# Attention and two expert layers on one core: joined float32 groups, another opening order, and weight forms held behind a unit's evictions

## The chip, the cores and the metric

The program runs on one NeuronCore of one Trainium2 chip. The metric is the device time of one execution in microseconds (us). TensorE (PE; its weight loads are PEld), VectorE (DVE), ScalarE (ACT), GpSimd (POOL) and SyncE (SP, which issues nearly all DMAs) each take their instructions in order from a queue of their own.

## The reference, cut to what matters

```python
B, H, S, D, NP = 8, 8, 576, 64, 32
def sm_attn(qq, kk, vv):                 # per batch and head
    a = softmax(qq @ kk.T / 8)
    return a @ vv
pp = sm_attn(p, k, v)                    # 32 packed rows per head
x  = sm_attn(q, pp, pp)                  # 576 rows, as (4608, 512)
x  = ((x @ w1) * (x @ w2)) @ w3 @ w_out  # 512 -> 1024 -> 1024 -> 512
h  = x @ w_in                            # 512 -> 2048
out = maximum(0.01 * h, h) @ moe2_w_out  # 2048 -> 512
```

The weights of both expert layers come as float64, all else as float32.

## The kernel before

**Two ways to multiply.** The large products run in a fast type, float32r, as three products of a high and a low part: hi*hi, hi*lo, lo*hi (`three`, line 128, and `run`, line 741). ACT makes the high part as a copy (CAST), DVE the low part as a difference (`sub`, line 134). The small products of the attention and of M stay in float32: they use 64 rows and 32 columns of the array at a time (`eights`, line 159, which gives 8 matmuls that run side by side), or 128 rows and 32 columns (`pv_mm`, line 213).

**The opening.** `word`, `bits` and `join` (lines 273 to 291) turn float64 words into float32: ACT one instruction, DVE two, POOL one for each tile of 128x512. Sixteen tiles of w3, eight of w_out and sixteen of w1 and w2 are converted. `w13_mm` multiplies w3 and w_out beforehand: 64 products of 512 columns into eight sums W13. Batch 0's attention and the first pieces of its expert layer run among them. The order of all this is written out by hand in the table `SCRIPT` (line 11): one word is one step, and each engine meets its instructions in that order. `l` is a load of a tile to convert (512 KB), `c`, `b`/`B`, `j` are its ACT, DVE and POOL steps, `w.fc.jc` a product of W13, `k`, `q`, `v`, `p` loads of the attention, `s`, `S` its two score products, `t` transposes, `y` the product with v, `M.b.f` the weights times packed rows, `A.b.fc.th` a piece of the expert layer. Loads go into three tiles of their own, then into two buffers of M, round and round (`conv_load`, line 303).

**The body, batches 1 to 7.** A batch is 24 pieces (`pieces`, line 476): 16 `ab_unit` of 12 matmuls of 288 columns and 8 `x2_unit` of 24. The steps of the next batch's attention are hung behind pieces by number (`attention`, line 486; `rest_of_m`, line 513): scores behind piece 2, transposes behind 5 and 6, the product with v behind 9 and 11, one M behind pieces 21, 0, 4 and 8. M is f = 0 to 3 for each batch. A scheduler puts the instructions of an engine in its own order, but float32 matmuls of one group stay together (`together`, line 116).

**The last layer.** 18 units t of 768 tokens, in three parts F of d_ff (3, 3 and 2 blocks). A product is done with seven multiplications instead of eight (`sevens`, line 696), so inputs and weights are first turned into seven forms (`form`, line 528), each with a high and a low part. `h_unit` makes h, `g_ops` its forms, `o_unit` the output (one unit later). Each eviction of a sum is `first` or `add`. With every new F the forms of w_in (`make_wi`, line 644) and w_out (`make_wo`) are made again. In the last unit of a part `o_unit` runs twice in succession. Outputs of F = 0 and 1 go to DRAM (`part`) and come back into the output tiles `o` (six buffers, `begin_o`, line 789).

```python
for mb in range(2):
    for i in range(2):
        o = b2.tile([P, 2, HT], F32, tag="o", name="o", bufs=OB)
...
for x in (1, 3, 0, 2):
    nc.sync.dma_start(out=todo[x][1], in_=todo[x][0])
...
if end:
    begin_o(t)
    o_unit(t)
    if t + 1 < TB:
        make_wi(F + 1)
```

Of the kernel before, what the change touches and what calls it, by code (L numbers as in the profile page):

```python
# [11 lines left out]
l.3.0 l.o.1 l.o.2 l.o.0 l.o.4 l.o.3 l.3.1 v.0.1 c.3.0 B.3.0 p.0 v.0.0 j.3.0 c.o.1 B.o.1 l.3.4 k.0.1 k.0.0 j.o.1 c.o.2  # L12
B.o.2 l.o.5 p.1 w.0.1 j.o.2 l.3.2 c.o.0 B.o.0 w.0.2 j.o.0 l.3.6 c.o.4 B.o.4 w.0.0 j.o.4 l.3.3 c.o.3 B.o.3 j.o.3 l.o.6
c.3.1 B.3.1 w.0.3 j.3.1 l.3.5 w.0.4 c.3.4 B.3.4 j.3.4 l.o.7 w.2.1 w.2.0 s.0 c.o.5 B.o.5 w.2.3 q.0.1 m.0.0 j.o.5 c.3.2
w.2.2 l.3.8 B.3.2 e.0.0 q.0.0 w.0.5 p.2 c.3.6 t.0.0 B.3.6 j.3.2 l.3.12 T.0.0 B.3.3 w.1.0 j.3.6 l.3.10 c.3.3 w.1.2
c.o.6 n.0.0 j.3.3 l.3.7 B.o.6 w.1.3 c.3.5 w.1.1 m.0.1 j.o.6 l.3.13 w.1.4 c.o.7 B.o.7 w.1.5 e.0.1 w.0.6 B.3.5 j.o.7
y.0.0 n.0.1 j.3.5 l.3.11 t.0.1 l.3.9 Y.0.0 B.3.8 c.3.8 w.1.6 T.0.1 w.2.4 j.3.8 l.w.1 y.0.1 w.2.6 Y.0.1 v.1.0 B.3.12
c.3.12 w.0.7 v.1.1 w.1.7 j.3.12 c.3.10 B.3.10 wh.0 w.2.7 l.3.15 wh.1 wl.0 j.3.10 l.3.14 w.2.5 c.3.7 B.3.7 w.3.3 wh.2
c.3.13 w.3.1 B.3.13 j.3.7 l.w.2 w.3.0 c.3.11 B.3.11 w.3.7 j.3.13 l.w.3 w.3.5 c.3.9 B.3.9 j.3.11 l.w.0 w.3.2 w.3.6
c.w.1 wl.1 j.3.9 z.0 B.w.1 w.3.4 Z.0 S.0 wh.3 wl.2 j.w.1 l.w.4 wl.3 w.4.0 D.0.0 k.1.1 w.4.3 k.1.0 w.4.4 c.3.15 w.4.1  # L20
B.3.15 E.0.0 w.5.4 c.3.14 B.3.14 j.3.15 l.w.5 w.6.7 l.w.6 c.w.2 w.5.2 D.0.1 j.3.14 w.4.6 c.w.3 w.4.7 w.6.2 c.w.0 B.w.3
# [34 lines left out]
def tile_kernel(ctx, tc, qT, kT, vL, pT, w12, w3b, wo1, win, wo2, out):  # L56
# [77 lines left out]
    def sub(engine, out, x, hi):  # L134
        engine.tensor_tensor(out=out, in0=x, in1=rd(hi), op=ALU.subtract)  # L135
# [48 lines left out]
    def s1_exp(b, g):  # L184
        st = stats[b, g]
        pt = att.tile([P, S], F32, tag="P", name="P", bufs=2)
        nc.scalar.activation(
            out=pt.rearrange("p (a s) -> p a s", a=2), in_=s1q[b][g][:, :, :TH], func=AF.Exp, bias=st[:, 1:2],
            scale=SCALE, accum_out=st[:, 2:3],
        )  # L190
        Ps[b, g] = pt
# [6 lines left out]
    def t_mm(b, g):  # L198
        pt = Ps.pop((b, g))
        t = ps_at()  # L200
        for c in range(4):
            nc.tensor.transpose(t[:, 0, c * P:(c + 1) * P], pt[:, c:512:4], ident)  # L202
        nc.tensor.transpose(t[:64, 1, :P], pt[:, 512:576], ident)
        PTs[b, g] = t

    def t_copy(b, g):
        t = PTs[b, g]
        PT = att.tile([P, 5, P], F32, tag="PT", name="PT", bufs=2)
        nc.scalar.copy(PT[:, 0:4].rearrange("p c s -> p (c s)"), t[:, 0])
# [93 lines left out]
    def conv_load(key, i):  # L303
        n = 0
        if key != "w" or i < 4:
            n = loads[0] % (C64 + 4)
# [584 lines left out]
```

## Time and profile before

| | |
|---|---|
| runs | 1295.27 us median of 3 (1294.71 to 1297.86) |
| the profiled execution | 1297.09 us, span of its instructions 1295.3 us |
| mean granted clock of TensorE | 0.996 |
| busy | PE 97%, PEld 90%, DVE 67%, ACT 47%, POOL 8% |
| opening with batch 0 | about 0 to 126 us |
| batches 1 to 7 | to about 575 us |
| last layer | to 1292 us |

The page gives busy time by engine. The chain of waits follows the end of the program back through what released each instruction. The timeline lists instructions in order of time, with the idle time ahead of one and what ended it. Sums by stretches give each engine's busy time in a window with the granted clock (1.00 is 2.4 GHz, 0.50 is 1.2 GHz). A row of a float32 matmul is one of two passes, so it counts twice: 64 products of W13 are 128 rows.

### The profile page before, as it was taken

The numbers are of one execution on the slowest core, as the hardware profiler recorded it, in microseconds if no ns is written. First come the engines' busy times: TensorE is split into PE (matmuls) and PEld (weight loads), VectorE is DVE, ScalarE is ACT, GpSimd is POOL, SyncE is SP. The second block draws the span as 40 slices with busy tenths as digits, with TensorE's granted clock in tenths as the row PEclk, the third lists the DMA queues.
The fourth block names the chain that finished last, engine by engine and source line by source line (L and its number), as shares of the span: only waits on it lengthen the run. The fifth ranks groups of instructions, "written<-read, shape, count | busy, mean of one in ns | idle before, by whom it ended". The sixth has DMA issues, their size and how long they took to land.

```text
span 1295.3 us, 23350 instructions
## 1 busy us (share of the span) xinstructions
PE 1262.9 (97%) x8984; PEld 1170.3 (90%) x8984; DVE 870.8 (67%) x1449; ACT 609.3 (47%) x1141; POOL 102.4 (8%) x87
## 2 busy tenths in 40 slices
PE   5989999999999999999999999999999998999998
PEld 2458998989898989999999999999999998999998
DVE  5887465676766767648866774676457549586667
ACT  3445344454545454546565555454433343443342
POOL 4543011111110101000000000000000000000000
PEclk9999999999999999999999999999999999999999
DMA  9944244566665745468789776484754583878873
GB/s 351 350 154 160 66 159 140 194 218 220 208 219 164 242 137 187 144 216 273 256 306 318 279 255 219 130 285 147 268 198 144 195 283 105 310 267 294 303 258 122
DMA packets 139375, 283.08 MB, mean 219 GB/s; under 512 B 14848, under 2 KB 66048, under 8 KB 139264
## 3 DMA queue, kind: packets, MB, share of 16 engines
q1 hardware_dynamic: 130048, 272.16, 61.2%
q10 hardware_dynamic: 9216, 9.44, 2.2%
q8 instruction: 70, 1.15, 0.4%
q14 instruction: 41, 0.34, 0.1%
HBM read 202.38 MB, written 79.17 MB: 217 GB/s over the span
## 4 chain that ended last, share of the span: by engine, by line
PE 87%; DMA 8%; DVE 2%; issue 1%; SPq 1%; ACT 1%; POOL 0%; ACTq 0%; DVEq 0%; POOLq 0%
PE mm L130 30%; PE b L746 28%; PE c L746 14%; PE a L746 7%; PE mm L379 4%; PE at L163 4%; DMA xh<-xfd 2%; DMA xfd<-xt 1%; DMA v<-vL 1%; PE at L221 1%; PE at L202 0%; DMA raw<-kT 0%; DMA xfd<-xr 0%; DMA wi<-wid 0%; DMA xfd<-P 0%
## 5 line engine op out<-in xcount | busy, mean ns | idle before, releaser
L130 PEld LDWEIGHTS mm<-AT,M 128*128 128x128 f32 x1536 | 207.9, 189 | 30.2 <-issue 11.7
L130 PE MATMUL mm<-AT,M 128*128 128x288 f32 x1536 | 223.5, 300 | 3.8 <-DVE M L135 2.9
L746 PE MATMUL b<-xh,wi 128*128 128x384 f32 x768 | 219.1, 335 | 0.0
L746 PE MATMUL b<-gh,wo 128*128 128x384 f32 x768 | 214.1, 335 | 3.4 <-DVE o L704 2.7
L130 PEld LDWEIGHTS mm<-ab,W 128*128 128x128 f32 x1536 | 203.5, 188 | 8.3 <-ACT x2s L454 4.2
L130 PE MATMUL mm<-ab,W 128*128 128x288 f32 x1536 | 207.4, 295 | 0.0
L746 PEld LDWEIGHTS b<-gh,wo 128*128 128x128 f32 x768 | 140.3, 188 | 4.7 <-DVE o L704 3.3
L746 PEld LDWEIGHTS b<-xh,wi 128*128 128x128 f32 x768 | 141.0, 188 | 0.3 <-ACT gr L706 0.2
L746 PE MATMUL b<-gl,wo 128*128 128x384 f32 x384 | 128.4, 334 | 0.7 <-DVE gl L135 0.7
L746 PE MATMUL b<-xl,wi 128*128 128x384 f32 x384 | 128.4, 334 | 0.0
L746 PE MATMUL c<-xh,wi 128*128 128x384 f32 x384 | 107.6, 339 | 3.8 <-DMA xh<-xfd 3.8
L539 ACT CAST gh<-gr 128x1152 fp32r<-128x1152 f32 (+1 forms) x72 | 75.5, 1052 | 69.0 <-PE b L746 56.6
L746 PE MATMUL c<-gh,wo 128*128 128x384 f32 x384 | 106.9, 335 | 0.9 <-DVE o L704 0.9
L433 DVE TENSOR_TENSOR ab<-mm,a 128x288 f32<-128x288 f32 x128 | 57.8, 454 | 60.7 <-PE mm L130 40.6
L135 DVE TENSOR_TENSOR gl<-gr,gh 128x1152 fp32r<-128x1152 f32 (+1 forms) x72 | 87.5, 1220 | 11.5 <-ACT gh L539 11.4
L539 ACT CAST gh<-gs 128x1152 fp32r<-128x1152 f32 (+1 forms) x54 | 56.8, 1053 | 57.3 <-PE b L746 31.7
L135 DVE TENSOR_TENSOR ab<-ab,ab 128x288 fp32r<-128x288 f32 x119 | 59.8, 507 | 31.4 <-ACT ab L438 29.6
L694 ACT ACTIVATE gr<-gr 128x1152 f32<-128x1152 f32 (+1 forms) x54 | 57.3, 1062 | 47.0 <-DVE gr L709 46.8
L438 ACT CAST ab<-ab 128x288 fp32r<-128x288 f32 x128 | 55.0, 432 | 50.9 <-DVE ab L433 50.8
L746 PEld LDWEIGHTS c<-xh,wi 128*128 128x128 f32 x384 | 70.9, 190 | 5.1 <-DMA xh<-xfd 4.2
L379 PE MATMUL mm<-ab,w 128*128 128x512 f32 x128 | 61.6, 635 | 14.1 <-POOL ab L290 9.6
L746 PEld LDWEIGHTS b<-gl,wo 128*128 128x128 f32 x384 | 72.1, 188 | 1.0 <-DVE gl L135 1.0
(119 smaller groups left out, 2020.6 us busy)
## 6 DMA issues: line engine op xcount, KB each, us to landing
xh<-xfd SPq DMA_DIRECT2D x126, 384.0 KB, 5.7
xl<-xfd SPq DMA_DIRECT2D x126, 384.0 KB, 5.4
part<-o SPq DMA_DIRECT2D x48, 384.0 KB, 3.0
o<-part SPq DMA_DIRECT2D x48, 384.0 KB, 4.1
c<-wo SPq DMA_DIRECT2D x20, 512.0 KB, 5.2
xfd<-xt SPq DMA_DIRECT2D x49, 192.0 KB, 3.1
xfd<-xr SPq DMA_DIRECT2D x49, 192.0 KB, 2.8
raw<-kT SPq DMA_DIRECT2D x32, 288.0 KB, 5.7
```

The lines of the kernel that those rows point to most:

```text
L130: ins = nc.tensor.matmul(dst, lhs(i), rhs(j), start=first and n == 0, stop=last and n == 2)
L135: engine.tensor_tensor(out=out, in0=x, in1=rd(hi), op=ALU.subtract)
L163: ins = nc.tensor.matmul(dst(h)[c * 32:c * 32 + 32], lhs[r, c, :], rhs(c)[r], start=True, stop=True)
L221: ins = nc.tensor.matmul(ps[r, :64], PT[:K, c, r], v[:K, c, g * 64:g * 64 + 64], start=c == 0, stop=c == 4)
L379: nc.tensor.matmul(w13p[fc], words["3", i][:, c:c + P], words["o", jc], start=w13n[fc] == 1, stop=w13n[fc] == 8)
L433: nc.vector.tensor_tensor(out=t, in0=pb[:, :TH], in1=a, op=ALU.mult)
L438: nc.scalar.copy(t[:, 0], ab32[fc, th])
L539: nc.scalar.copy(hi[step], x[step])
L694: nc.scalar.activation(out=out, in_=x, func=AF.Prelu, alpha=0.01)
L746: nc.tensor.matmul(dst, lhs(l), rhs(r), start=first and n == 0, stop=last and n == total - 1, skip_group_check=True)
```

## The change

1. **Joined groups.** `m_pair` issues M for f and f+1 as one float32 group, behind pieces 21 and 4. `t_mm` and `pv_mm` of the two halves g become one group each (behind pieces 7 and 10); scores move from behind piece 2 to 1. The last 64 tokens of v and P get zeros behind them (POOL memsets), so that every matmul of `pv_mm` uses 128 rows, and `t_copy` is one ACT instruction in place of two. M has three buffers in place of two.
2. **A new table `SCRIPT`.** The same steps in another order; loads may use six halves of M.
3. **Forms of w_in.** The loads (`load_wi`) are apart from the forms (`make_wi`). In the last unit of a part the forms' DVE instructions may not stand ahead of an eviction of `o_unit`: for a = 0 the one at a quarter of its DVE evictions, for a = 1 the one at half. For F = 0 they wait in the same manner for the low part of piece 12 of batch 7 (before: loaded and made behind piece 9). Forms of unit 2's second half start behind piece 17, not 11.
4. **Outputs.** Output tiles are taken in the order in which the unit first writes them, and the last unit's four stores are eight halves.

```diff
 SCRIPT = """
-l.3.0 l.o.1 l.o.2 l.o.0 l.o.4 l.o.3 l.3.1 v.0.1 c.3.0 B.3.0 p.0 v.0.0 j.3.0 c.o.1 B.o.1 l.3.4 k.0.1 k.0.0 j.o.1 c.o.2
...
+l.3.1 l.o.5 l.3.5 l.o.4 l.o.6 l.3.7 l.o.3 l.o.7 k.0.0 c.3.1 B.3.1 c.o.5 B.o.5 j.3.1 l.o.2 c.3.5 B.3.5 k.0.1 j.o.5
...
             nc.sync.dma_start(out=t[:64, 4], in_=src[512:576])
+            nc.gpsimd.memset(t[64:, 4], 0.0)
...
-        pt = att.tile([P, S], F32, tag="P", name="P", bufs=2)
+        pt = att.tile([P, 5 * P], F32, tag="P", name="P", bufs=2)
+        nc.gpsimd.memset(pt[:, S:], 0.0)
...
-                    ps[r, :64], PT[:K, c, r], v[:K, c, g * 64:g * 64 + 64], start=c == 0, stop=c == 4
+                    ps[r, :64], PT[:, c, r], v[:, c, g * 64:g * 64 + 64], start=c == 0, stop=c == 4
                 )
-                together(ins, c + j == 0)
+                together(ins, g + c + j == 0)
...
-            n = loads[0] % (C64 + 4)
+            n = loads[0] % (C64 + 6)
...
-    def m_unit(b, f):
+    def m_pair(b, f):
         m_mm(b, f)
-        m_hi(b, f)
-        m_lo(b, f)
+        m_mm(b, f + 1, False)
+        for x in (f, f + 1):
+            m_hi(b, x)
+            m_lo(b, x)
...
     def rest_of_m(b):
-        return {4 * f - 4: [lambda f=f: m_unit(b, f)] for f in range(1, 4)}
+        return {4: [lambda: m_pair(b, 2)]}
...
+        def gate(engine, ins):
+            if behind and engine in behind:
+                after(ins, behind[engine])
...
-        for mb in range(2):
-            for i in range(2):
+        for i in range(2):
+            for mb in range(2):
...
-        for x in (1, 3, 0, 2):
-            nc.sync.dma_start(out=todo[x][1], in_=todo[x][0])
+        for x in (2, 3, 0, 1):
+            for j in ((slice(0, 1), slice(1, 2)) if t == TB - 1 else (slice(0, 2),)):
+                nc.sync.dma_start(out=todo[x][1][:, j], in_=todo[x][0][:, j])
...
             begin_o(t)
+            del evicted[:]
             o_unit(t)
             if t + 1 < TB:
-                make_wi(F + 1)
+                n = len(evicted)
+                load_wi(F + 1)
+                make_wi(F + 1, ({"v": evicted[n // 4]}, {"v": evicted[n // 2]}))
```

What the change moves is seen at three places.

First TensorE in the body, from the second scores of one batch to the product with v of the next. `at<-w,ppT` is M (x8 is one f), `at<-raw,pks` the first scores, `at<-ident,P` transposes, `at<-v,PT` the product with v. Before:

```order
L130 MATMUL mm<-ab,W_76 128x288 x120
L163 MATMUL at<-w,ppT_77 32x512 x8
L130 MATMUL mm<-AT,M 128x288 x12
L163 MATMUL at<-raw,pks_80 32x288 x16
L202 MATMUL at<-ident,P 128x128 x4
L203 MATMUL at<-ident,P 64x128
L130 MATMUL mm<-AT,M 128x288 x18
L221 MATMUL at<-v,PT 32x64 x20
```

Now:

```order
L130 MATMUL mm<-ab,W_76 128x288 x120
L164 MATMUL at<-w,ppT_77 32x512 x16
L130 MATMUL mm<-ab,W_76 128x288 x48
L164 MATMUL at<-raw,pks_80 32x288 x16
L130 MATMUL mm<-AT,M 128x288 x36
L164 MATMUL at<-w,ppT_77 32x512 x16
L205 MATMUL at<-ident,P 128x128
L221 MATMUL at<-v,PT 32x64 x40
```

Rows that repeat are left out. M stood in 31 groups of the program (30 of one f, one of two) and stands in 18 (14 of two, four of one); the product with v stood in 16 groups of one half and stands in nine, seven of them of both halves.

Second SyncE at the start: `c_...` and `M` are tiles to convert, `w3b` is w3, `wo` w_out. Before:

```order
L315 DMA c_88<-w3b 128x1024
L315 DMA c_90<-wo 128x1024
L315 DMA M<-wo 128x1024 x3
L315 DMA M<-w3b 128x1024
L155 DMA v<-vL 128x512
L156 DMA v<-vL 64x128
L315 DMA c_126<-w3b 128x1024
L148 DMA raw<-kT 128x576 x4
```

Now:

```order
L315 DMA c_88<-w3b 128x1024
L315 DMA c_90<-wo 128x1024
L315 DMA c_92<-w3b 128x1024
L315 DMA M<-wo 128x1024 x2
L315 DMA M<-w3b 128x1024
L315 DMA M<-wo 128x1024 x2
L148 DMA raw<-kT 128x576 x2
L315 DMA M<-wo 128x1024
L148 DMA raw<-kT 128x576 x2
```

A tile of w_out gives products only with a tile of w3 of the same half: the even ones (3.0, 3.4) with o0 to o3, the odd ones (3.1, 3.5, 3.7) with o4 to o7. Before, the first seven tiles were 3.0, o1, o2, o0, o4, o3 and 3.1, the eighth came behind four pairs of loads of v, and k behind that. Now the first eight are 3.1, o5, 3.5, o4, o6, 3.7, o3 and o7, then come two pairs of k around o2, and v only behind twelve tiles.

Third VectorE where F goes from 1 to 2: `gr` and `o` are evictions of h and of the output, `xr` and `wi` the forms of w_in, `gl` forms of h. Before:

```order
L709 TENSOR_TENSOR gr<-c,gr 128x384 x2
L535 TENSOR_TENSOR xr<-wi_6933,wi_6934 128x256
L535 TENSOR_TENSOR xr<-xr,wi_6929 128x256
L535 TENSOR_TENSOR xr<-wi_6929,wi_6933 128x256
L135 TENSOR_TENSOR wi_6934<-wi_6934 128x256
L709 TENSOR_TENSOR gr<-c,gr 128x384
L135 TENSOR_TENSOR wi_6931<-xr,wi_6931 128x256
L704 TENSOR_TENSOR o<-b,o 128x384
```

Now:

```order
L717 TENSOR_TENSOR o<-a,o 128x384
L545 TENSOR_TENSOR xr<-wi_6964,wi_6965 128x256
L717 TENSOR_TENSOR o<-b,o 128x384
L135 TENSOR_TENSOR gl<-gs,gh 128x1152
L717 TENSOR_TENSOR o<-c,o 128x384
L545 TENSOR_TENSOR xr<-xr,wi_6960 128x256
L135 TENSOR_TENSOR wi_6965<-wi_6965 128x256
```

The 22 forms stood ahead of the last eviction of h and of all evictions of the next two output units; now they stand among the evictions of the second of these units.

## Rows read from the trace of the kernel before

**Rows 1.** Page, part 1: busy us, share of the span, instructions.
```profile
PE 1262.9 (97%) x8984; PEld 1170.3 (90%) x8984; DVE 870.8 (67%) x1449; ACT 609.3 (47%) x1141; POOL 102.4 (8%) x87
```

**Rows 2.** Chain of waits, opening and 210 to 280 us: start, us, what.
```profile
53.00 27.68 PE mm L379 x64
...
212.75 1.02 PE at L163 x16
213.77 3.37 PE mm L130 x24
217.14 1.13 PE at L163 x32
...
224.44 0.47 PE at L202 x4
224.91 0.11 PE at L203
...
233.18 0.83 PE at L221 x40
234.01 3.40 PE mm L130 x24
...
249.22 16.00 PE mm L130 x120
```

**Rows 3.** Timeline, TensorE, 8.5 to 31 us: start, us, work, idle before.
```profile
8.91 5.49 PE L379 MATMUL mm<-ab,w 128*128 128x512 f32 x6 [8.91 <-POOL ab L290]
...
21.21 3.63 PE L379 MATMUL mm<-ab,w 128*128 128x512 f32 x4 [3.44 <-POOL w L290]
```

**Rows 4.** Sums by stretches: length, busy PE, PEld, DVE, ACT, POOL, clock, DMA share, GB/s.
```profile
8.90:30.00 21.10, 15.90 (x58) 5.55 (x58) 12.07 (x19) 6.72 (x12) 10.14 (x8) 0.92 1.00 373
30.00:83.00 53.00, 52.62 (x258) 22.95 (x258) 47.05 (x78) 24.09 (x44) 28.69 (x22) 1.00 0.75 272
...
86.28:89.67 3.39, 3.39 (x14) 3.39 (x15) 2.62 (x5) 1.02 (x3) 1.35 (x2) 0.50 0.56 162
...
858.00:861.00 3.00, 3.00 (x11) 3.00 (x11) 2.57 (x4) 1.16 (x1) 0.00 (x0) 0.50 0.88 347
1074.00:1080.00 6.00, 5.05 (x28) 4.41 (x27) 6.00 (x11) 2.58 (x3) 0.00 (x0) 1.00 0.01 1
```

**Rows 5.** Timeline, TensorE, 82 to 92 us.
```profile
82.07 1.09 PE L163 MATMUL at<-w,ppT 64*32 64x512 f32 x16 [0.38 <-DVE W L135]
...
86.28 4.69 PE L130 MATMUL mm<-AT,M 128*128 128x288 f32 x22 [2.66 <-DVE M L135]
```

**Rows 6.** Groups by line and shape: busy us, mean ns, idle before.
```profile
L135 DVE TENSOR_TENSOR M<-at,M 128x1024 fp32r<-128x1024 f32 x32 | 39.1, 1224 | 20.7 <-ACT M L401 20.7
...
L401 ACT CAST M<-at 128x1024 fp32r<-128x1024 f32 x32 | 32.4, 1013 | 5.4 <-PE at L163 3.0 <-ACT x2s L454 1.2 <-PE mm L130 0.4
...
L280 DVE TENSOR_SCALAR ct<-M 128x512 uint32<-128x512 uint32 x16 | 11.1, 694 | 0.4
```

**Rows 7.** Timeline, TensorE, 1066 to 1086 us: the rows with idle time.
```profile
1073.24 0.44 PE L746 MATMUL b<-gh,wo 128*128 128x384 f32 x1 [2.05 <-DVE o L704]
...
1077.37 0.44 PE L746 MATMUL c<-gh,wo 128*128 128x384 f32 x1 [0.57 <-DVE o L704]
...
1079.77 0.44 PE L746 MATMUL c<-gh,wo 128*128 128x384 f32 x1 [0.38 <-DVE o L704]
...
1082.31 0.44 PE L746 MATMUL b<-gl,wo 128*128 128x384 f32 x1 [0.69 <-DVE gl L135]
```

**Rows 8.** Timeline, VectorE, 1060 to 1073 us.
```profile
1067.00 0.42 DVE L535 TENSOR_TENSOR xr<-wi,wi 128x256 f32<-128x256 f32 x1 [3.55 <-DMA wi<-wid]
...
1072.63 0.55 DVE L704 TENSOR_TENSOR o<-b,o 128x384 f32<-128x384 f32 x1
```

**Rows 9.** Timeline, TensorE, 853 to 860 us.
```profile
856.20 0.44 PE L746 MATMUL c<-xh,wi 128*128 128x384 f32 x1 [1.89 <-DMA xh<-xfd]
```

**Rows 10.** DMA issues, 1280 to 1296 us: count, KB each, median us to landing.
```profile
out<-o SPq DMA_DIRECT2D x5, 384.0 KB, 2.3
```

More of the change, by code (lines that the diff above doesn't have):

```diff
@@ L17 @@
[L17 to L21, printed above, removed]
@@ L134, in sub @@
     def sub(engine, out, x, hi):
-        engine.tensor_tensor(out=out, in0=x, in1=rd(hi), op=ALU.subtract)
+        return engine.tensor_tensor(out=out, in0=x, in1=rd(hi), op=ALU.subtract)
     raws, vs, Ps, PTs, stats, ATs = {}, {}, {}, {}, {}, {}
@@ L442, in ab_lo @@
         t = abt[fc, th]
-        sub(engine, t[:, 1], ab32.pop((fc, th)), t[:, 0])
+        mark["v"] = sub(engine, t[:, 1], ab32.pop((fc, th)), t[:, 0])
     def x2_mm(b, th, e):
@@ L490, in attention @@
         d[1] += [lambda: load_v(b, 1)]
-        d[2] += [lambda: s1_mm(b)]
+        d[1] += [lambda: s1_mm(b)]
         for g in range(2):
-            d[2] += [lambda g=g: s1_max(b, g)]
-            d[3] += [lambda g=g: s1_exp(b, g)]
-            d[4] += [lambda g=g: s1_norm(b, g)]
-            d[4 + g] += [lambda g=g: load_kq("q", b, g)]
-            d[5 + g] += [lambda g=g: t_mm(b, g), lambda g=g: t_copy(b, g)]
-            d[9 + 2 * g] += [lambda g=g: pv_mm(b, g), lambda g=g: pv_scale(b, g)]
-        d[12] += [lambda: pp_mm(b), lambda: pp_copy(b)]
+            d[1] += [lambda g=g: s1_max(b, g)]
+            d[2] += [lambda g=g: s1_exp(b, g)]
+            d[3] += [lambda g=g: s1_norm(b, g)]
+            d[3 + g] += [lambda g=g: load_kq("q", b, g)]
+            d[7] += [lambda g=g: t_mm(b, g)]
+        for g in range(2):
+            d[7] += [lambda g=g: t_copy(b, g)]
+            d[10] += [lambda g=g: pv_mm(b, g)]
+        for g in range(2):
+            d[10] += [lambda g=g: pv_scale(b, g)]
+        d[13] += [lambda: pp_mm(b), lambda: pp_copy(b)]
         d[16] += [lambda: s2_mm(b)]
@@ L534, in form @@
                 new = sum_of(m, x.get(m))
-                nc.vector.tensor_tensor(out=new, in0=x[a], in1=x[b], op=op)
+                gate("v", nc.vector.tensor_tensor(out=new, in0=x[a], in1=x[b], op=op))
                 x[m] = new
@@ L632, in tile_kernel, with form_w @@
     wi = {m: b1.tile([P, 2, 2, 384], F32R, name=f"wi{m}") for m in ORDER}
-    def form_w(w, size):
+    def form_w(w, size, behind=None):
         for c in range(0, size, HT):
@@ L641, in form_w, with load_wi @@
                 lambda m, x: rd(b1.tile([P, HT], F32R, tag="xr", name="xr", bufs=XR))[:, :s.stop - s.start],
+                behind=behind,
             )
-    def make_wi(F):
+    def load_wi(F):
         m0, n = PARTS[F]
@@ L650, in make_wi @@
                 nc.sync.dma_start(out=rd(wi[m])[:, 1, a, :P * n].rearrange("p (m c) -> p m c", m=n), in_=src)
-            form_w({m: (wi[m][:, 0, a], wi[m][:, 1, a]) for m in ORDER}, P * n)
+    def make_wi(F, behind=(None, None)):
+        for a in range(2):
+            form_w({m: (wi[m][:, 0, a], wi[m][:, 1, a]) for m in ORDER}, P * PARTS[F][1], behind[a])
     xops = {}
@@ L666, in stage_b @@
         return stage(u, a, lambda: rd(tile("xr", XR)), lambda: rd(tile("xr", XR)), lambda: tile("xt", XT))
-    fill = {9: [lambda: make_wi(0)], 10: [lambda: load_forms(0, ORDER[:4])]}
-    slots(last, fill, spread(stage_b(2, 1), 11, 23))
+    fill = {
+        9: [lambda: load_wi(0)], 10: [lambda: load_forms(0, ORDER[:4])],
+        12: [lambda: make_wi(0, (dict(mark), dict(mark)))],
+    }
+    slots(last, fill, spread(stage_b(2, 1), 17, 23))
     stA.close()
@@ L739, in sevens, with run @@
                         first(dst(1, 0), B[x], old)
-    def run(dst, pairs, first, last):
+    def run(dst, pairs, first, last, in_turn=False):
         total = 3 * len(pairs)
@@ L810, in product @@
                     [(lambda l, c=c: wo[m][:, l, c, mb * P:mb * P + P], lambda l, c=c: G[m][l][:, c]) for c in range(n)],
[L811 removed]
+                    first, last, False,
                 )
[L814 removed]
+            chains.append((product, lambda i, j, mb=mb: todo[2 * i + mb][0][:, j], F > 0))
         sevens(chains, None)
[L816 to L817 removed]
+        for x in (2, 3, 0, 1):
+            for j in ((slice(0, 1), slice(1, 2)) if t == TB - 1 else (slice(0, 2),)):
+                nc.sync.dma_start(out=todo[x][1][:, j], in_=todo[x][0][:, j])
     load_forms(0, ORDER[4:])
```

82 lines of the change are left out of this document (43 added, 39 removed).

## The prediction, made before the change was run

> **What bounds the kernel now.** I read the page's busy times first: TensorE is busy 1262.9 us of 1295.3, VectorE 67%, GpSimd 8% [rows 1]. A change can gain only by taking work or overhead from TensorE's own row, or by closing the 32 us in which it stands. The chain of waits tells which: it runs through TensorE nearly everywhere, so a gap ahead of a float32 group and behind it is time of the program [rows 2]. The timelines then show the few places where TensorE waits for something else: in the opening for converted tiles [rows 3], at 83 us for the low part of M on VectorE [rows 5], where F goes from 1 to 2 for evictions [rows 7], at 856 us for a DMA [rows 9]. The sum is made against the profiled execution, 1297.09 us; the median of the runs shown is 1.8 below it. About 0.3% (3.9 us) is what a measurement of this kernel can tell from no change.
>
> **Joined groups: -8.8 us (bounds -6.2 and -8.8).** First what a group costs beyond its matmuls. 120 fast matmuls take 16.00 us, 0.1333 each, so 24 take 3.20; behind a float32 group 24 take 3.37, which adds 0.17 to the group before them [rows 2]. M of one f is 8 matmuls in 2 passes (x16), run side by side as 2 sets of 512 columns: 1.02 + 0.17 = 1.19 us. A score group is 4 sets of 288 columns: 1.13 + 0.17 = 1.30 [rows 2]. So 128 columns more cost 0.11 us, 0.86 ns a column; M's content is 1024 x 0.86 = 0.88 us and 1.19 - 0.88 = 0.31 is paid once per group.
> M goes from 31 groups to 18: 13 x 0.31 = 4.0 us.
> The product with v of one batch half is 0.83 + 0.20 = 1.03 us, since the 24 matmuls behind it took 3.40 [rows 2]. Its content is 20 matmuls in 10 sets of 64 columns: 10 x 64 x 0.86 = 0.55 us; overhead 0.48, more than a group's 0.31. Within it the shape changes too, from 128 rows to 64 rows for the last tokens. With zeros behind these the shape stays. Two halves cost 2.06 now and 2 x 0.55 + 0.31 = 1.41 joined: 0.65 saved, seven times, 4.5; the two groups left single save 0.17 each, 0.3 more. If the 0.17 is not the change of shape, seven joins give 7 x 0.31 = 2.2, which is the low bound. I take 4.8: the change of shape is the one thing in this group that those of the scores and of M lack.
> No row shows the two shapes apart. The Trainium skill, TensorEngine Tiling (Array Packing), section Key Properties, says that changing the tiling mode, though not the tile within a mode, drains the engine. By it the term is 4.8, without it 2.2.
> Transposes: 0.47 + 0.11 = 0.58 us for five sets [rows 2], 0.116 each, the same as the single fifth one, so all of it is content and joining them saves nothing.
>
> **The opening: -6 us (bounds -1 and -10).** Between 8.90 and 30 us TensorE is busy 15.90 of 21.10 [rows 4], 5.2 us idle: 3.44 of it in one piece ahead of 21.21, waiting for a converted tile of w [rows 3]. A product row is 27.68 / 64 = 0.4325 us at full clock [rows 2]. The first six rows take 5.49 where full clock would be 2.60: the engine starts at half clock, and that stays. The four rows at 21.21 take 3.63 instead of 1.73 and some work behind them is slow too: about 2.4 lost to the half clock that follows the idle 3.44. So 7.6 us is what an opening without holes would give.
> Does the new order have none? Tiles are 512 KB and the queue moved 373 GB/s (DMA share 1.00) [rows 4], 1.4 us a tile; VectorE needs 2 x 0.694 = 1.39 us for each [rows 6]. So a tile about every 1.5 us, the second ready near 8.9. In the old order the tiles give 1, 2, 3, 3, 4, 5 and, behind the loads of v, 9 products; in the new one 1, 2, 4, 6, 9, 9, 12 (two of w3 instead of one meet each w_out). Four products at half clock take 3.5 us, about two tiles' time. From the fourth tile on (about 12 us) TensorE always has work, and 12 products with the scores behind them carry it past the point where k has landed. I count the whole 7.6.
> What is new on the other side: fewer idle slots mean the same 59 us of VectorE's work (12.07 + 47.05 of 74) [rows 4] have to fit into about 68, 87% busy. In the order the product w.5.7 now opens a fifth sum while fc 0, 2 and 3 still hold theirs, so it stands behind the low part of a W13 sum on VectorE, which stands behind a conversion: 1.4 + 0.6 less what TensorE has in between, 1.5 us. The wait of 2.66 for M's low part and the 3.39 us at half clock behind it [rows 4, 5] stay, since two conversions stand ahead of it in both orders. 7.6 - 1.5 = 6. Bounds: nothing but the half clock given back and a new hole of 1.5 (-1); all holes closed, also that at 83 us (-10).
>
> **Where F goes from 1 to 2: -3.2 us (bounds 0 and -3.7, and +2).** TensorE waits 2.05 + 0.57 + 0.38 + 0.69 = 3.7 us there [rows 7]. VectorE has waited 3.55 for the load of wi, with evictions of the output queued behind the forms; the first eviction comes at 1072.63 [rows 8], and after that VectorE is busy 6.00 of 6.00 [rows 4]. In the new order the first four of the 14 evictions of the second output unit go ahead. What then remains for VectorE is 10 evictions of 0.55 (5.5), 22 forms of at most 0.42 (9.2) and two low parts of about 1.35 (2.7; from 1.224 for 1024 columns [rows 6], scaled), 17 us at most, some of them overlapping at the start. TensorE's 126 matmuls of 384 columns are 126 x 0.1333 x 384 / 288 = 22 us, 10/14 of which is 16. The two nearly meet; I keep 0.5 as a rest. The +2 is a unit t + 1 that wants its forms while VectorE is still at them. Where F goes from 0 to 1 TensorE has no idle row now and I cost it at 0 (up to +1.5 by the same argument). The forms behind piece 12 instead of 9 of batch 7 stand beside TensorE's pieces: 0.
>
> **Outputs: -1.5 us (bounds 0 and -3.6) and -0.4 us (bounds -0.1 and -0.5).** At 856 TensorE waits 1.89 us for the DMA of xh [rows 9] and then runs some 3.4 us at half clock [rows 4], 1.7 more. On SP two loads of o from `part` stand ahead of that xh load, each behind a store that has to land; with tiles taken by need one stands there. One landing is about 2.3 us [rows 10], enough for 1.89, but the order on SP shows one wait still ahead of it, so I count 1.5 of 3.6. The last store, 384 KB, takes 2.3 us from issue to landing [rows 10]; 0.39 MB at 373 GB/s is 1.05 us, and halves let the first one go earlier: 0.4 of the 0.5.
> The Trainium skill, DMA: Bandwidth & Descriptors, puts a fixed cost of about 2.0 us on a transfer, mostly completion. By it the halves would save about 0.15. Either way the sum moves by less than 0.3.
>
> **New waits at the joined groups: +1 us (bounds 0 and +16).** Behind M for f = 2 and 3 (piece 4) both `at` buffers are taken until M is copied: a high part of 1.01 and two low parts of 1.22 [rows 6], 3.5 us with other rows of VectorE between. Transposes stand 36 matmuls further on, 4.8 us, which covers it. Where two evictions and a further conversion slip in, VectorE could need 7.5: 2.7 us, in each of six batches 16. I take 1. The POOL memsets cost 0, POOL is 8% busy [rows 1] and they stand far ahead of their readers. The scores behind piece 1 in place of 2 cost 0: their operands are loaded a batch earlier.
>
> **Sum.** -8.8 - 6 - 3.2 - 1.5 - 0.4 + 1 = -18.9: 1278.1 for the profiled execution, 1276 against the median.
>
> **The rivals.**
> 1. The opening gains nothing: loads (share 1.00) or VectorE at 87% set its end, and closed holes open again before 83 us. For it: [rows 4], 47.05 of 53.00 on VectorE already. Against it: TensorE has 52.62 of 53.00 there and is ahead of nothing. 1276 + 6 = 1282. Chance 0.15.
> 2. Overheads are not what I took them for: the 64-row change costs nothing (-2.2 in place of -4.8), and the forms come late where F changes (0 in place of -3.2). 1276 + 2.6 + 3.2 = 1282. Chance 0.14.
> 3. The change doesn't do what it says: groups that the scheduler takes apart again. The order shows them joined; then only the front and the outputs count, about 1285. Chance 0.03.
> 4. Slower. Transposes behind the double M wait 2.7 us in each batch, and the clock falls to half behind each wait: 3.39 us of work at 0.50 [rows 4] cost 1.7. 4.4 x 6 = 26, so 1276 + 26 = 1302. It decides from 19 / 6 = 3.2 us a batch. For it: the clock fell after waits of 2.66 and 1.89 us [rows 4, 5, 9]. Against it: after 2.05 us at 1073.24 it stayed at 1.00 [rows 4, 7], and 4.8 us of matmuls cover 3.5. Chance 0.05. The Trainium skill, TensorE: Matmul & The Clock Gate, section What's actually happening, makes the slow clock the default, which activity lifts. By that rule every wait could cost its clock and the time would be this rival's; the row at 1074 does not bear it out.
>
> **How the numbers follow.** My forecast has 0.63, the rivals 0.15, 0.14, 0.03 and 0.05. The range takes in the forecast with its terms at their bounds (all holes closed, -4; new waits, +3) and rivals 1 and 2 with some of each other's loss: 1267 to 1288. Faster by over 0.3% are all cases but the fourth and a share of mixed mishaps: 0.91; within 0.3%: 0.04; slower: 0.05.
>
> **What would show it right or wrong.** Rows of M with x32 at about 1.02 + 0.88 = 1.9 us, of the product with v with x80 at 1.2 to 1.3 us (1.6 would be the low bound). In the opening no idle row over 1 us between 12 and 30 us and TensorE's chain reaching the second batch's scores 6 us earlier. Around F = 2 idle rows of TensorE of 0.5 in all, VectorE's forms among evictions. At 856 no idle row and no stretch at 0.50. Transposes behind M with no idle row, or rival 4 with 2 us or more on `at`. The forecast is wrong if TensorE's busy time falls by less than 6 us, or the opening has a new wait over 3 us.

## The result and the profile after

| | before | changed |
|---|---|---|
| median, us | 1295.07 of 4 runs (1294.71 to 1297.86) | 1274.83 of 4 runs (1272.55 to 1277.70) |
| ratio | | 0.984 (95% interval 0.9815 to 0.9866) |
| profiled execution, its span | 1297.09, 1295.3 | 1277.70, 1275.6 |

The forecast was 1276 us in 1267 to 1288. The profiled execution of the changed kernel is the slowest of its four; the same kernel, run again later, gave 1276.22 us (six runs, 1272.00 to 1278.91) with a ratio of 0.9844 (0.9822 to 0.9865). Its ten runs lie 7 us apart; part of why is among the findings.

The page after the change, part 1 (busy us, share, instructions). TensorE has lost 13.6 us of busy time with the same 8984 matmuls [rows 1]; 6 us more were idle time.

```profile
PE 1249.3 (98%) x8984; PEld 1169.9 (92%) x8984; DVE 870.6 (68%) x1448; ACT 610.3 (48%) x1125; POOL 113.2 (9%) x136
```

Where the 19.7 us of the two spans went. The first two lines are the start of the same matmul in the two traces; the others are TensorE's time beyond its pitch (0.1734 us for 384 columns), summed over the matmuls of that stretch. The last column is a second profiled execution of the changed kernel (span 1275.0, from the later run).

| stretch | predicted | measured | second execution |
|---|---|---|---|
| opening, to the 128th matmul `mm<-AT,M` (111.76, now 103.51) | -6 | -8.3 | -7.5 |
| from there to the first matmul of h (575.43, now 558.68) | -8.8 + 1 | -8.5 | -9.0 |
| F = 0, and F from 0 to 1 (beyond pitch 0.9, now 1.9) | 0 | +1.0 | -0.1 |
| start of F = 1, xh (3.8, now 4.1) | -1.5 | +0.3 | -2.7 |
| rest of F = 1, and F from 1 to 2 (5.7, now 0.3) | -3.2 | -5.4 | -5.4 |
| F = 2 (6.4, now 7.7) | 0 | +1.3 | +4.7 |
| behind the start of the last matmul (4.10, now 3.90) | -0.4 | -0.2 | -0.2 |

Two executions of one program differ in single stretches of the last layer by 3 us, and much of that cancels in the sum. What holds in both is the opening, the body and the step from F = 1 to 2.

**The groups.** The chain of waits of the changed kernel, one batch (start, us, what), in answer to [rows 2]:

```profile
150.62 1.88 PE at L164 x32
152.50 4.98 PE mm L130 x36
157.48 0.47 PE at L204 x4
157.95 0.11 PE at L205
158.06 0.48 PE at L204 x4
158.54 0.11 PE at L205
158.65 4.76 PE mm L130 x36
163.41 1.25 PE at L221 x80
164.66 3.38 PE mm L130 x24
```

M of two f is one row of 1.88 us (1.9 was said) and 36 matmuls behind it take 4.98 instead of 36 x 0.1333 = 4.80: 2.06 in all, where two groups took 2 x 1.21 (the mean over the batches; 1.19 in the row that the prediction used), so 0.35 saved. Both halves of the product with v take 1.25 (1.24 was said) + 0.19 = 1.44, where they took 2 x 1.03 [rows 2]: 0.62. The transposes are still 0.58 for each half: nothing saved. No idle row stands at them, though M takes both `at` buffers just ahead of them: the 36 matmuls cover the copies of M, as the 4.8 us said.

**The opening.** Timeline of TensorE, changed kernel, 8 to 84 us, the first row and the rows with idle time (start, us, work, idle before), in answer to [rows 3, 5]:

```profile
8.69 13.68 PE L379 MATMUL mm<-ab,w 128*128 128x512 f32 x24 [8.69 <-POOL ab L290]
22.30 1.20 PE L164 MATMUL at<-raw,pks 64*32 64x288 f32 x32
...
38.24 2.81 PE L379 MATMUL mm<-ab,w 128*128 128x512 f32 x6 [1.23 <-DVE W L135]
75.64 1.95 PE L164 MATMUL at<-w,ppT 64*32 64x512 f32 x32 [1.50 <-DVE W L135]
77.94 0.53 PE L130 MATMUL mm<-AT,M 128*128 128x288 f32 x2 [0.35 <-ACT M L401]
80.00 3.18 PE L130 MATMUL mm<-AT,M 128*128 128x288 f32 x22 [1.52 <-DVE M L135]
```

Twelve products run without a hole and the scores follow at 22.30, as the walk along the tiles had it. The new wait at the fifth sum is there too, 1.23 us for VectorE's low part of W13 (1.5 was said). Around M's matmuls TensorE now waits 1.50 for the low part of W13 (0.38 before) and 1.52 for that of M (2.66 before) [rows 5].

Sums by stretches, changed kernel (columns as in rows 4):

```profile
8.69:22.30 13.61, 13.46 (x24) 5.19 (x25) 11.10 (x17) 5.40 (x8) 9.89 (x10) 1.00 1.04 404
80.00:83.40 3.40, 3.40 (x35) 3.15 (x42) 3.33 (x5) 1.94 (x4) 1.33 (x2) 1.00 0.56 166
841.04:843.50 2.46, 2.46 (x8) 2.46 (x9) 1.69 (x3) 1.17 (x1) 0.00 (x0) 0.50 1.02 410
1104.00:1106.00 2.00, 2.00 (x8) 2.00 (x7) 2.00 (x6) 1.32 (x5) 0.00 (x0) 0.50 1.03 415
```

Behind M the clock stays at 1.00 here (second line), where it was 0.50 at this place before [rows 4]: 1.7 us that the sum had not counted. Behind two waits for xh it is 0.50 (the last two lines).

**F from 1 to 2.** Timeline of VectorE, changed kernel, in answer to [rows 8]:

```profile
1077.36 0.55 DVE L717 TENSOR_TENSOR o<-a,o 128x384 f32<-128x384 f32 x1
1077.83 0.42 DVE L545 TENSOR_TENSOR xr<-wi,wi 128x256 f32<-128x256 f32 x1
1078.36 0.56 DVE L717 TENSOR_TENSOR o<-b,o 128x384 f32<-128x384 f32 x1
```

Evictions pass between forms, and TensorE has no idle row from 1048 to 1098 us; the four of [rows 7] are gone. (In the trace of before eight of the 22 forms stood ahead of the last eviction of h, 15 ahead of the first eviction of the output, and seven among these, not all 22 ahead of them.)

**The waits for xh are not gone.** Timeline of TensorE, and then of SP ahead of the first of the two waits, with the landing of its load of 834.12:

```profile
841.04 0.69 PE L765 MATMUL c<-xh,wi 128*128 128x384 f32 x1 [2.46 <-DMA xh<-xfd]
...
1102.82 0.44 PE L765 MATMUL c<-xh,wi 128*128 128x384 f32 x1 [2.27 <-DMA xh<-xfd]
```

```profile
825.53 0.92 SPq L839 DMA_DIRECT2D part<-o  x1
829.97 0.32 SPq L819 DMA_DIRECT2D o<-part  x1
830.34 0.45 SPq L674 DMA_DIRECT2D xh<-xfd  x1
...
831.81 0.32 SPq L819 DMA_DIRECT2D o<-part  x1
...
834.12 0.42 SPq L674 DMA_DIRECT2D xh<-xfd  x1
```

```profile
DMA to landing us min/median/max: 6.9/6.9/6.9
```

SP stands from 826.4 to 830.0 at a load of o, and the loads of xh are behind it. By the list of SP's waits such loads wait for a store to land, one from whose tile the new one takes its buffer: 32.9 us in 21 waits for `part`, up to 4.4 us. But the load that TensorE waited for, that of 834.12, was not held by these: it followed on a load of xl whose buffer TensorE had only just freed, 11.3 us into the unit of h. It landed 6.9 us later, and between its issue and its landing five loads landed: the o of 829.97 and an xh and an xl behind it, the o of 831.81, and the xl just ahead.

**The tail.** DMA issues of the changed kernel, 1262 to 1276 us, in answer to [rows 10]:

```profile
out<-o SPq DMA_DIRECT2D x8, 192.0 KB, 1.9
```

Half the bytes land in 1.9 us instead of 2.3, and the end moved by 0.2.

### The profile page after: what moved, and what is told of

Read it like the earlier page. It is cut to its first block, busy times and chain, and to the rows that moved or that the text cites. A ratio compares the mean times of both kernels' runs of the same rounds, so it can differ in the third digit from the quotient of the medians.

```text
span 1275.6 us, 23472 instructions
## 1 busy us (share of the span) xinstructions
PE 1249.3 (98%) x8984; PEld 1169.9 (92%) x8984; DVE 870.6 (68%) x1448; ACT 610.3 (48%) x1125; POOL 113.2 (9%) x136
## 4 chain that ended last, share of the span: by engine, by line
PE 92%; DMA 6%; DVE 2%; ACT 0%; issue 0%; SPq 0%; DVEq 0%; ACTq 0%
PE mm L130 32%; PE b L765 30%; PE c L765 15%; PE a L765 7%; PE at L164 4%; PE mm L379 3%; DMA xh<-xfd 2%; DMA M<-w3b 1%; PE at L221 1%; DMA c<-w3b 1%; PE at L204 1%; DMA xfd<-xr 1%; DMA xr<-x2d 0%; DVE cT L283 0%; DMA v<-x2d 0%
## 5 line engine op out<-in xcount | busy, mean ns | idle before, releaser
L130 PE MATMUL mm<-AT,M 128*128 128x288 f32 x1536 | 215.2, 297 | 3.6 <-DVE M L135 1.5
L717 DVE TENSOR_TENSOR o<-b,o 128x384 f32<-128x384 f32 x108 | 59.1, 553 | 31.4 <-PE b L765 30.9
L135 DVE TENSOR_TENSOR ab<-ab,ab 128x288 fp32r<-128x288 f32 x119 | 54.7, 460 | 33.5 <-ACT ab L438 32.0
L765 PEld LDWEIGHTS b<-xl,wi 128*128 128x128 f32 x384 | 72.2, 188 | 0.0
```

The lines of the kernel that those rows point to most:

```text
L130: ins = nc.tensor.matmul(dst, lhs(i), rhs(j), start=first and n == 0, stop=last and n == 2)
L135: return engine.tensor_tensor(out=out, in0=x, in1=rd(hi), op=ALU.subtract)
L717: evicted.append(nc.vector.tensor_tensor(**args))
L765: ins = nc.tensor.matmul(dst, lhs(l), rhs(r), start=first and n == 0, stop=last and n == total - 1, skip_group_check=True)
```

## The experiments

Ratios are against the kernel before, run on the same chip.

**The opening undone.** `SCRIPT` and the four halves of M as before, all else as changed.

```diff
-            n = loads[0] % (C64 + 6)
+            n = loads[0] % (C64 + 4)
```

> The changed kernel with the opening's order of before (the old table, loads in four halves of M; M of batch 1, f = 1, is then one single group behind piece 0, 0.35 us). Theory (the opening is worth what the traces show at its end): the 128th matmul of the first fast kind came at 103.51 us with the change and at 111.76 before, 8.25 earlier. Undoing the table gives that back: 1274.8 + 8.25 + 0.35 = 1283 us, with TensorE idle some 3.4 us ahead of 21 us, a wait of about 2.7 us between the first fast matmuls behind M and a granted clock near 0.50 behind it. Rival (the lead at 100 us comes from joined groups and less from the order, or is given back later): 1277 us or less.

Measured: 1284.79 us (1284.14 to 1286.87), ratio 0.9921 (0.9902 to 0.9940), 10 us more than the changed kernel. The hole in TensorE's timeline, and the clock behind it:

```profile
21.82 3.78 PE L379 MATMUL mm<-ab,w 128*128 128x512 f32 x4 [3.68 <-POOL w L290]
```

```profile
21.00:27.00 6.00, 5.18 (x32) 1.83 (x36) 1.38 (x2) 1.34 (x2) 2.14 (x3) 0.50 0.99 387
```

The 128th matmul starts 9.6 us later than with the new table, and 1.3 later than in the kernel before, whose table this is: the old order is a little slower still beside the other parts. So the opening is worth 8 to 10 us and none of it is given back later. The rival with a full VectorE falls: 58.97 us of its work stand in the 66.95 us to 75.64, 88%, and three waits of 1.2, 1.5 and 1.5 us are all that it costs.

**The groups split again**, the zeros kept.

```diff
-    def m_pair(b, f):
-        m_mm(b, f)
-        m_mm(b, f + 1, False)
+    def m_unit(b, f):
+        m_mm(b, f)
...
-                together(ins, g + c + j == 0)
+                together(ins, c + j == 0)
```

> The changed kernel with every float32 group split again and hung where it was before (M of one f behind pieces 21, 0, 4 and 8, transposes and the product with v by halves, scores behind piece 2); the zeros behind the last 64 tokens stay. Theory: a group costs about 0.35 us beyond its content (two groups of M 2 x 1.208 against 2.062 joined), so M gives back 13 x 0.35 = 4.6, the product with v 7 x 0.35 = 2.5, less 0 to 2 of waits that came with the new places: 1274.8 + 5 to 7 = 1280 to 1282 us. The group of one half of the product with v, all of 128 rows now, takes 0.90 us of TensorE (0.35 + half of 1.44 - 0.35) where the one with a tail of 64 rows took 1.02: then the change of shape cost 0.12. Rival for the shape: it takes 1.02 as before, and padding is worth nothing. Rival for the groups: no more than 1277 us, since waits of other engines take the place of the overhead.

Measured: 1281.76 us (1279.43 to 1287.60), ratio 0.9907 (0.9878 to 0.9935), 6.9 more. The chain of waits of this kernel:

```profile
206.06 1.02 PE at L164 x16
207.07 3.37 PE mm L130 x24
...
226.49 0.70 PE at L221 x40
227.18 3.39 PE mm L130 x24
```

A half of the product with v, all of 128 rows, takes 0.70 + 0.19 = 0.89 us; with the tail of 64 rows it took 0.83 + 0.20 = 1.03 [rows 2]. In this group the only difference is the tail's shape: 0.14 us (0.17 was said). From 0.89 single and 1.44 joined follow 0.55 of content and 0.34 per group, the same as M's 0.35. So of the 0.62 that a join saves, 0.34 is a group less and 2 x 0.14 the shape kept. The Trainium skill, TensorEngine Tiling (Array Packing), section Key Properties, says that a change of tiling mode drains the engine; the trace agrees, with 0.34 us for a group between full-size matmuls and 0.14 us for 64 rows inside a group of 128.

**No gate for the forms of w_in** (F = 1 and 2).

```diff
-                make_wi(F + 1, ({"v": evicted[n // 4]}, {"v": evicted[n // 2]}))
+                make_wi(F + 1)
```

> The changed kernel without the rule that holds the forms of w_in behind a quarter and a half of the evictions (F = 1 and 2; that of F = 0 stays). Theory: where F goes from 1 to 2 the forms stand ahead of the evictions again and TensorE waits 2.2 + 0.7 + 0.5 + 0.9 = 4.3 us as it did before; the 1.1 us which TensorE waits now where F goes from 0 to 1 go. 1274.8 + 3 = 1278 us. Rival: the earlier loads of w_in (ahead of the forms of the whole unit) were what mattered, and the order on VectorE costs nothing: 1274 to 1275 us.

Measured: 1276.82 us (1275.30 to 1281.06), ratio 0.9869 (0.9843 to 0.9894): 2 more than the first runs of the changed kernel and 0.6 more than the later ones, which the intervals do not separate. The trace does, though of the slowest of four executions (1281.06, the others to 1276.90); TensorE, 1030 to 1066 us, has waits at the evictions again that the changed kernel lacks:

```profile
1038.04 0.44 PE L765 MATMUL b<-xh,wi 128*128 128x384 f32 x1 [1.84 <-ACT gr L725]
1059.85 0.44 PE L765 MATMUL c<-gh,wo 128*128 128x384 f32 x1 [0.57 <-DVE o L717]
1062.25 0.44 PE L765 MATMUL c<-gh,wo 128*128 128x384 f32 x1 [0.37 <-DVE o L717]
1064.78 0.44 PE L765 MATMUL b<-gl,wo 128*128 128x384 f32 x1 [0.68 <-DVE gl L135]
```

3.5 us there; beyond the pitch the rest of F = 1 takes 5.4 us, as before the change (5.7), where both executions of the changed kernel have 0.3. Against it stand the 1.1 us where F goes from 0 to 1, which are gone without the gate; the second execution of the changed kernel has 0.3 of them. So the gate does at F = 2 what it was made for and costs up to 1.1 us at F = 1; how much of it is left in the time these medians don't settle.

**The outputs in the old order, whole last stores.**

```diff
-        for i in range(2):
-            for mb in range(2):
+        for mb in range(2):
+            for i in range(2):
```

> The changed kernel with the output tiles taken in the order of before, and whole last stores. Theory by the traces: the order of the tiles has not removed the waits for xh (2.63 and 2.44 us with it against 2.05 and 1.50 before), so undoing it changes nothing there beyond 1 us either way, and the tail gets 0.2 to 0.4 longer: 1274.8 + 0.3, within 1274 to 1276 us. Rival (as the prediction had it: one load of o fewer ahead of xh is worth 1.5): with the old order the waits for xh grow by 1.5 us or more each: 1278 us.

Measured: 1277.68 us (1274.68 to 1278.20), ratio 0.9859 (0.9839 to 0.9879). TensorE waits 5.9 us for xh in four places, against 5.1 in three of the changed kernel; nothing like 1.5 each. SP meets the loads of o and xh at the start of F = 1 in the same order as with the new order of tiles. Whether the new order is worth the 1.5 to 2.9 us between the medians (the later and the first runs of the changed kernel) or nothing stays open, since the intervals overlap.

**Loads of xh on GpSimd.**

```diff
-                nc.sync.dma_start(out=rd(xops[t, m][l]), in_=src)
+                nc.gpsimd.dma_start(out=rd(xops[t, m][l]), in_=src)
```

> The changed kernel with the loads of xh and xl issued by GpSimd, which does nothing in the last layer, in place of SP. Theory: SP takes its transfers in turn, and the stores of output tiles wait there for their evictions (167.8 us in 43 waits, up to 18.6 us), with loads of xh behind them; the waits of TensorE for xh of 2.63 us at 838 and 2.44 us at 1100, each with a stretch of half clock behind it (1.5 us each), go: 1274.8 - 7 = 1268 us. Rival: the DMA engines themselves are the limit there (share 0.93 to 0.99 from 825 to 840 us), the waits stay or move: 1273 to 1276 us. A second rival: GpSimd issues its transfers more slowly and new waits for xh come up: over 1276 us.

Measured: 1288.45 us (1286.12 to 1301.83), 14 more. What TensorE waits for in the last layer (us, times, longest):

```profile
PE b L765 <- ACT gr L725: 6.3, 4, 3.6
PE b L765 <- DVE gr L717: 4.6, 2, 3.8
PE c L765 <- DMA xh<-xfd: 1.5, 2, 0.9
```

The wait for xh fell from 5.1 to 1.5 us, as the theory had it, and longer waits came up on other engines; 13 of the 14 us lie in F = 0, where the changed kernel hardly waits. The scheduler had ordered these engines anew; which of their waits comes from that and which from the transfers wasn't tried.

**Stores on GpSimd instead** (the same edit at `out=todo[x][1]`).

> The changed kernel with the stores of output tiles issued by GpSimd in place of SP, the loads of xh on SP as they are. Theory: stores that wait for evictions no longer hold up loads of xh, and GpSimd's transfers stand in nobody's way: 1274.8 - 7 = 1268 us. Rival: what made the run with the form loads on GpSimd 13 us slower (TensorE waiting 6.3 us for ACT and 4.6 us for VectorE on gr, once xh was in time) was the new order of the other engines' instructions, which comes with any transfer moved to GpSimd: new waits for gr, over 1276 us.

Measured: 1274.10 us (1273.50 to 1274.63), ratio 0.9837 (0.9817 to 0.9858): no change. The rival's waits for gr didn't come, but the waits for xh stay at 4.3 us. Stores that wait on SP for their evictions are not what makes xh late.

**Loads of o behind those of xh, on SP.**

```diff
+                    if hold:
+                        after(ins, newest[0])
...
-            begin_o(t - 1)
+            begin_o(t - 1, True)
```

> The changed kernel with one rule more: the loads of o from part for a unit's outputs stand behind the last load of xh and xl of the unit of h that runs beside it, on SP. Theory: the waits for xh at 838 and 1100 us come from SP, which stands at a load of o until a store has landed (826.4 to 830.0, and 1098.9 to 1100.9) while loads of xh are behind it; with these ahead the waits of 2.63 and 2.44 us and the half clock behind each (1.5 us) go: 1274.8 - 8 = 1267 us, more likely 1268 to 1270 as the loads of o come later. Rival: the DMA engines are full there (share 0.93 to 0.99), xh is late anyway: 1274 to 1276 us.

Measured: 1270.31 us (1269.41 to 1271.40), ratio 0.9807 (0.9789 to 0.9825); all its runs lie below all ten of the changed kernel. The wait at 838 is gone, with its half clock, and no wait of TensorE for xh is left in the last layer (5.1 us before the change, 5.1 and 4.8 in the two executions of the changed kernel). SP, with the landing of its load of 832.30, the one that was late in the changed kernel:

```profile
822.00 1.10 SPq L843 DMA_DIRECT2D part<-o  x2
826.35 0.32 SPq L676 DMA_DIRECT2D xl<-xfd  x1
...
832.30 0.38 SPq L676 DMA_DIRECT2D xh<-xfd  x1
```

```profile
DMA to landing us min/median/max: 3.8/3.8/3.8
```

Sums by stretches, of the changed kernel (first line) and of this one:

```profile
829.00:837.00 8.00, 8.00 (x48) 8.00 (x47) 8.00 (x18) 5.89 (x15) 0.00 (x0) 1.00 0.99 341
829.00:837.00 8.00, 8.00 (x48) 8.00 (x47) 8.00 (x18) 5.88 (x12) 0.00 (x0) 1.00 0.59 178
838.00:846.00 8.00, 8.00 (x48) 8.00 (x47) 6.68 (x9) 5.48 (x7) 0.00 (x0) 1.00 0.99 383
```

The load leaves SP as far into its unit of h as in the changed kernel, 11.3 us, and lands 3.8 us later instead of 6.9. So SP did not hold this load: what cost the time was the transfers ahead of it. TensorE comes to it some 15.7 us into the unit, which leaves 4.4 us for its landing: 6.9 is 2.5 too many, the 5.2 of the changed kernel's second execution 0.8 too many, 3.8 in time. With the rule the loads of o come behind it, and the pair of xl and xh that stood behind one of them leaves 2 us sooner in its unit; the share of the DMA engines ahead of it is 0.59 instead of 0.99, and they are full only later (last line). The rival was right that the engines were full, and wrong that xh is late anyway.

The second wait stays in another form; ACT, and then TensorE:

```profile
1092.82 0.71 ACT L549 CAST wo<-wo 128x384 fp32r<-128x384 f32 x2 [4.79 <-DMA wo<-wod]
1093.44 0.47 ACT L727 COPY gr<-b 128x384 f32<-128x384 f32 x1
```

```profile
1093.96 0.69 PE L767 MATMUL b<-xh,wi 128*128 128x384 f32 x1 [3.15 <-ACT gr L727]
```

ACT stands at a form of w_out that has not landed, an eviction of gr behind it.

**That wait, tried in four ways**: the forms of w_out behind half or all of the evictions of the unit of h, the stores on GpSimd, and both.

```diff
-            make_wo(F)
+            make_wo(F, {"v": evicted[len(evicted) // 2], "a": copied[len(copied) // 2]} if t else None)
```

> The kernel with the loads of o held behind xh, and one rule more: the forms of w_out for F = 1 and 2 stand behind half of the evictions of the unit of h beside them, on VectorE and on ACT. Theory: what is left there is ACT, which stood 4.8 us at a form of w_out whose load had not landed, with evictions of gr behind it; TensorE waited 3.3 us at 1090 us and ran 6.6 us at half clock behind it (3.3 more). With the forms behind: 1270.3 - 6 = 1264 us. Rival: the loads come late as a whole (o, w_out and xh share the DMA engines there), the wait moves to the first product that needs w_out: 1268 to 1271 us.

> The same with the forms of w_out behind all evictions of that unit of h. Theory: as good as half, since a whole unit of h (some 20 us) stands between these forms and their first reader: 1264 us. Rival: 14 us of forms on VectorE then come beside the next unit's evictions and reach the output unit late: 1266 to 1270 us.

> The kernel with the loads of o held behind xh, and the stores of output tiles issued by GpSimd. Theory: at the start of F = 2 SP still takes stores between the loads of xh and w_out (1080.4 to 1088.3 us) and stands at each; without them w_out and xh land some 2 us sooner, and of the 3.3 us wait and the half clock behind it (3.3) half goes: 1270.3 - 3 = 1267 us. Rival: the loads can't start before the unit of h frees their buffers, and from then on the DMA engines are full (share 0.95 from 1090 to 1095): 1269 to 1272 us.

> The same with the forms of w_out behind half of the evictions of the unit of h as well. Theory: neither ACT nor SP's stores are left ahead of xh: 1265 us. Rival: the wait is that of the loads themselves, 2 us at the third or fourth product of that unit: 1269 to 1272 us.

Measured: 1271.93 (ratio 0.9812, 0.9792 to 0.9833), 1272.62 (0.9823, 0.9801 to 0.9844), 1271.59 (0.9819, 0.9802 to 0.9837) and 1272.87 (0.9826, 0.9810 to 0.9842): none better than 1270.31. In each TensorE still waits 1.9 to 2.7 us at 1094 to 1097 us: for xh, or with all forms held for a form of w_out on ACT. TensorE and the sums of the third:

```profile
1096.62 0.42 PE L767 MATMUL c<-xh,wi 128*128 128x384 f32 x1 [2.10 <-DMA xh<-xfd]
```

```profile
1090.00:1095.00 5.00, 4.52 (x27) 4.20 (x25) 1.54 (x3) 3.32 (x7) 0.54 (x1) 1.00 0.95 289
1095.00:1100.00 5.00, 3.38 (x11) 3.41 (x12) 4.76 (x11) 3.30 (x8) 0.00 (x0) 0.69 1.02 414
```

From 1090 us the DMA engines are full. The rival holds at this place: xh and w_out come in together, and the order on ACT and SP only says which of them TensorE waits for. An explanation that fits is that the five buffers of xh come free only with the unit of h; more buffers weren't tried. In the sum of the kernel there is a second reason. Beyond pitch F = 2 takes 7.7 us with the loads of o held alone, and 7.1, 4.9, 5.4 and 6.7 in these four traces; but where forms of w_out are held TensorE waits 0.9 to 1.3 us at 860 us for a form of h on VectorE (1.2 to 3.7 us beyond pitch), and with stores on GpSimd the end comes 0.8 us later behind the last matmul.

**The changed kernel again.**

> The changed kernel itself again, on the chip of the two others, so that the three can be compared: 1273 to 1277 us, with waits for xh near 838 and 1100 us of 1 to 3.5 us which differ between executions.

Measured: 1276.22 us, as above. Its trace holds the same wait ahead of M's first matmuls as the first one, with another end (timeline of TensorE, then sums):

```profile
79.48 4.71 PE L130 MATMUL mm<-AT,M 128*128 128x288 f32 x22 [1.52 <-DVE M L135]
```

```profile
80.00:82.00 2.00, 2.00 (x11) 2.00 (x10) 1.93 (x5) 1.21 (x3) 0.24 (x1) 0.50 0.52 197
```

The same 1.52 us, and here half clock behind it: 22 matmuls take 1.5 us more than in the first execution. The waits for xh are 0.8, 2.1 and 1.9 us at 838, 1097 and 1185 here, 2.5, 2.3 and 0.3 at 838, 1100 and 1189 there. Differences of this size are what the runs of one kernel show among themselves.

## Why the prediction came out right

**The sum, term by term.** Joined groups: -8.8 said; 13 x 0.35 + 7 x 0.62 + 2 x 0.14 = 9.2 by the rows, and the run that split them (and kept the zeros) came back by 6.9 of 13 x 0.35 + 6 x 0.34 = 6.6. Each row of the joined kernel lies within 0.02 us of what the columns and the overhead gave. New waits at the groups: +1 said, 0 measured. Rival 4 had its place named and found nothing there; what came up is 1.0 us at 412, for an eviction behind a form that waits for its load on VectorE, and 0.7 at 531, where six forms of w_in on ACT stand ahead of a copy. The second of these is in both executions and belongs to a term that the sum put at 0, the forms behind piece 12. With these waits the body is 8.5 us shorter (9.0 in the second execution, which lacks the first wait), so 9.5 to 10 were gained there; by how much that exceeds the rows has not been taken apart.

The opening: -6 said, -8.3 measured, -7.5 in the second execution. 7.6 less 1.5 was the sum without the clock, and the wait of 1.23 was as foreseen. The step that was off is "the wait of 2.66 for M's low part and the 3.39 us at half clock behind it stay": M's wait fell to 1.52, that for the low part of W13 ahead of it grew from 0.38 to 1.50, so the two together stayed, and the half clock came in one execution and not in the other. Two more waits of before, 0.24 and 0.87 us at 97 and 100 us, went, which the sum had not named; with the old table they are back (0.23 and 1.00). F from 1 to 2: -3.2 said, -5.4 measured; all four rows are gone (3.7) and the rest of 0.5 is not there. The term was sized by idle time alone: behind each of these waits the next start came some 0.17 us later still, and about 1 us lay in delays that no row shows as idle. F from 0 to 1, costed at 0 with a bound of +1.5, gave +1.0 and, in the second execution, -0.1; F = 2, not in the sum, gave +1.3 and +4.7: its waits are much as before (4.5 us, now 4.3 and 5.7), but the clock fell to 0.50 behind one wait for xh, in the second execution behind two, and in the kernel before behind none. The tail: -0.4 said, -0.2 measured, between the low bound and the forecast; the run with whole stores has 4.12 again. The Trainium skill, DMA: Bandwidth & Descriptors, section Latency and other measured facts, speaks of a fixed cost of about 2 us; the estimate of 0.15 from it, (2.3 - 2.0) / 2, came nearer than the 0.4. The landings here, 1.9 us for half of the bytes and 2.3 for all, are below what that cost and the bytes would come to, and differ by 0.4.

**The step that failed** is the outputs: "with tiles taken by need one stands there", hence 1.5 of 3.6 us saved at 856. In the profiled execution the wait grew by 0.6 us and kept its half clock; in the second it was 0.8 us at full clock, and in the run with the old order 1.4. Over the last layer TensorE waited 5.1 us for xh before, 5.1 and 4.8 after. Between issue and landing of the late load two loads of o land after the change, as before it (issued at 846.13 and 847.44, the xh at 848.76). Nor is it the hold on SP that makes this load late, as the sum had it, but what lands ahead of it: 6.9 us from issue to landing (5.2 in the second execution), and 3.8 where the loads of o stand behind. The run that put them there took the wait away, and 4.5 us with it by the medians (5.9 against the later runs). The order of tiles alone moved nothing that the runs can tell.

**The chances.** Rival 1 (no gain in the opening) and both halves of rival 2 (no price of the shape, forms late) fell with the runs that undo the opening, the groups and the gate, rival 3 with the rows of joined groups. The median is 1.2 us below the forecast, and that it is so near is in part luck: the opening gained 2.3 us more than said and F from 1 to 2 2.2 more, the outputs 1.8 less, and F = 0 and F = 2 lost 1.0 and 1.3 that were not in the sum. In the second execution the outputs gained 1.2 more than said and F = 2 lost 4.7, with nearly the same sum.

## What to carry to other kernels

Price a small group in a row of large ones by two rows of different length: content by columns, and what is left is paid per group; then joining is plain arithmetic, and padding a tail so that the shape never changes was worth 0.14 us each time here. Before you count on a wait for a load going away, read when that load was issued and when it landed. If it was issued in time and landed late, ask what landed in between, and whether the edit puts that behind it. A wait of 1.5 us cost another 1.5 in clock here, in one execution and not in the other.

## What the runs showed of the chip that was not expected

- The same program, with the same 1.52 us wait, went on at 1.00 in one execution and at 0.50 in another.
- At the start the first six rows of W13 stand 0.85 us and more apart, twice their time, and the rest 0.43: 24 rows in 13.61 us [sums, 8.69 to 22.30], where 24 x 0.4325 = 10.38. The clock's column says 1.00 all the same, because the trace holds no granted clock before 14.5 us and the column counts such time as full. The starts of matmuls tell the speed there.
- A load of 384 KB took 3.8 us from issue to landing where the DMA engines had a share of 0.59 just ahead, and 6.9 us where it was 0.99. It was issued at the same place of its unit in both.
- A transfer issued by GpSimd took 0.54 us of that engine, and moving 252 loads there made the kernel 14 us slower though the loads came in time; moving the 76 stores of outputs changed nothing in the median, though the end behind the last matmul grew from 3.9 to 4.7 us.
